# Retention and a gelu MLP on one core: the first w_in part triggered earlier, M1 of the first chunk begun on two batches, two loads put ahead of the last w_out part

## Chip, cores and metric

The kernel runs on one NeuronCore of one Trainium2 chip. The metric is the device time of one execution in microseconds (us). Times inside the kernel are us from the start of the profiled span.

## What is computed

For 4 batches (`B`), 8 heads (`H`), 768 steps (`S`) and a head width of 64 (`D`), a retention recurrence with one decay per head, and then a two-layer MLP with a tanh gelu on the 3072 rows of width 512 that it gives:

```python
for t in range(S):
    state = gamma[None, :, None, None] * state + np.einsum('bhd,bhe->bhde', k[:, :, t], v[:, :, t])
    y[:, :, t] = scale * np.einsum('bhd,bhde->bhe', q[:, :, t], state)
x = np.ascontiguousarray(attn_out.transpose(0, 2, 1, 3)).reshape(B * S, H * D)
h = x @ w_in                                          # 512 x 2048
g = 0.5 * h * (1.0 + np.tanh(c * (h + 0.044715 * h * h * h)))
out = (g @ w_out).astype(np.float32)                  # 2048 x 512
```

All inputs and outputs are float32; the kernel works in float16 on the matmul side.

## The kernel before

**Chunks.** The 768 steps are cut into six chunks of 128. For each chunk and batch the recurrence becomes matmuls. `prep1` (L146) scales or casts a loaded 128x512 tile of q, k or v to float16, on the engine that is named in its first argument (VE = VectorE, AC = ScalarE, PO = GpSimd). `mm_T` (L183) transposes q and k of one batch on TensorE and `ev_T` (L192) copies the result out of PSUM. `mm_A` (L202) forms the scores and `ev_A` (L216) masks them, always on VectorE. `mm_yc`, `mm_yi` (L223, L238) form the outputs, `ev_Y` (L251) writes them as columns of the MLP's input x. `mm_s`, `ev_S` (L260, L274) carry the state to the next chunk. I call these steps T, A, Y and S. A chunk's x has 512 columns, 128 per batch.

**M1 and M2.** M1 is x times w_in and the gelu. It has 16 blocks of 128 features. `moe1` (L366) does one block on all 512 columns with four matmuls. `moe1_two` (L371) does a pair of blocks, `fp`, on a range of columns, so that it can start while later batches are not there yet: `t01` is batches 0 and 1, `t2` batch 2, `t3` batch 3. Each leaves its sum in a PSUM bank of the tag "h", of which there are two, and ScalarE takes it out with the gelu (L363). M2 is g times w_out, done with seven products of half size instead of eight, on sums of g and of w_out that VectorE or GpSimd form beforehand (`g_sums` L396, `w_sums` L389). For chunk 0 the products are cut into the pieces of `units_0` (L515), so that parts of w_out can be used as they arrive; a table (L734) says what work of chunk 1 is put after which piece.

**Weights.** w_in and w_out are each loaded in four parts. Each part is read as 1 MB of float32 and lands as 512 KB of float16. The loads are issued from GpSimd[...] (`load_w_in` L328, `load_w_out` L336). Part i of w_in holds blocks 4i to 4i+3; part i of w_out holds the same blocks of the second layer.

**Order.** There is no scheduler: each engine runs its instructions in the order in which the code records them (`manual_schedule`), and waits by semaphores. A DMA is issued by a queue's engine in that same order: `load1(AC, ...)` on ScalarE's, the loads of `nc.sync` on SyncE's, `load1(PO, ...)` and the weights on GpSimd's. Twelve loads of 256 KB bring q, k, v of the four batches of chunk 0; they are issued from SyncE and ScalarE in the first 10 us. `spin(n)` (L114) puts n matmuls on zeros into TensorE's queue, where it would otherwise have nothing to do.

**The opening.** After the twelve loads, GpSimd prepares k of batches 0 and 1, issues w_in part 0, prepares k of batch 2, issues w_in parts 1 to 3, prepares k and q of batch 3, issues the four parts of w_out and then loads of chunk 1 (`loads`, L604). TensorE does T, A, Y of batches 0 and 1, T and A of batch 2, T of batch 3, and then begins M1 with pair 0 on batches 0 and 1 (L672), with A, Y and S of the late batches between its pieces. From block 6 on, M1 goes by full blocks (L696).

Of the kernel before, what the change touches and what calls it, by code (L numbers as in the profile page):

```python
# [16 lines left out]
def kernel(  # L17
# [16 lines left out]
    NF = d_ff // 128  # L34
# [44 lines left out]
    def ld_tile(nm, c, b):  # L79
        if (nm, c, b) not in raw:  # L80
            raw[nm, c, b] = ld.tile([128, H, Dh], F32, tag=f"{nm}32", bufs=6 if nm == "v" else 8, name=f"{nm}32")
        return raw[nm, c, b]
# [31 lines left out]
    def spin(n):  # L114
        ps = bank("h", shape=(128, 512), name="spin_ps")
        for _ in range(n):
            nc.tensor.matmul(
                out=ps, lhsT=zero[:, 0:128], rhs=zero, start=True, stop=True
            )
# [20 lines left out]
    def copy_on(eng, out, in_):  # L140
        if eng is nc.scalar:
            eng.copy(out=out, in_=in_)  # L142
        else:
            eng.tensor_copy(out=out, in_=in_)

    def prep1(eng, nm, c, b):  # L146
        if nm == "v":
            t = pre.tile([128, H, Dh], F16, tag="v16", bufs=2 * B, name="v16")
        else:
            if (c, b) not in qk16:  # L150
                qk16[c, b] = pre.tile([128, 2, H, Dh], F16, tag="qk16", bufs=2 * B, name="qk16")
            t = qk16[c, b][:, "qk".index(nm)]
        src = ld_tile(nm, c, b)
        if (nm == "v") == (c < 1):
            copy_on(eng, t, src)
        else:
            col = OQ if nm == "q" else OK
            eng.tensor_tensor(  # L158
                out=t,
                in0=src,  # L160
                in1=cst[:, col:col + H].unsqueeze(2).broadcast_to([128, H, Dh]),
                op=ALU.mult,
            )
        h16[nm, c, b] = t

    def pair(t, hp):
        return t[:, 2 * hp:2 * hp + 2]
# [8 lines left out]
    def bank(tag, dt=F32, shape=(128, NHP, 128), name="ps"):  # L176
        return psum.tile(list(shape), dt, tag=tag, bufs=BANKS[tag], name=name)

    def qkT_tile(c, b):
        qkT[c, b] = att.tile([128, 2, NHP, 128], F16, tag="qkT", bufs=2 * B, name="qkT")  # L180
        return qkT[c, b]

    def mm_T(c, b):  # L183
        ps = bank("att", F16, (128, 2, NHP, 128), "qkT_ps")
        for i, nm in enumerate("qk"):
            for hp in range(NHP):
                nc.tensor.transpose(  # L187
                    out=ps[:, i, hp], in_=pair(h16[nm, c, b], hp), identity=iden
                )
        pss["T", c, b] = ps  # L190

    def ev_T(c, b, eng=nc.vector):  # L192
        copy_on(eng, qkT_tile(c, b), pss.pop(("T", c, b)))
# [8 lines left out]
    def mm_A(c, b):  # L202
        t = qkT[c, b]
        ps = [bank("att", name=f"a_ps{j}") for j in range(2)]
        for hp in range(NHP):
            for j in range(2):
                nc.tensor.matmul(  # L207
                    out=ps[j][:, hp],
                    lhsT=t[j * 64:(j + 1) * 64, 1, hp],
                    rhs=t[j * 64:(j + 1) * 64, 0, hp],  # L210
                    start=True,
                    stop=True,
                )
        pss["A", c, b] = ps

    def ev_A(c, b):  # L216
        ps = pss.pop(("A", c, b))
        for j in range(2):
            s = att.tile([128, NHP, 128], F16, tag=f"a{j}", name=f"a_sb{j}")
            nc.vector.tensor_tensor(out=s, in0=ps[j], in1=mask[:, j], op=ALU.mult)  # L220
            a_sb[c, b, j] = s

    def mm_yc(c, b, tag):  # L223
        y_ps = pss["Y", c, b] = bank(tag, name="y_ps")
        if c == 0:
            return

        for hp in range(NHP):
            nc.tensor.matmul(  # L229
                out=y_ps[:, hp],  # L230
                lhsT=st[:, b, hp].rearrange("p j d -> p (j d)"),
                rhs=qkT[c, b][:, 0, hp],
                start=(hp == 0),
                stop=False,
                skip_group_check=True,
            )
# [88 lines left out]
    NO = 4  # L325
    w_out_sb = [const.tile([128, NF // NO, d_model], F16, name=f"w_out{i}") for i in range(NO)]

    def load_w_in(i):  # L328
        nc.gpsimd.dma_start(
            out=w_in_sb[i],  # L330
            in_=moe_w_in.rearrange("(kc p) n -> p kc n", p=128)[
                :, :, w_in_at[i] * 128:(w_in_at[i] + w_in_n[i]) * 128
            ],
        )

    def load_w_out(i):  # L336
        n = NF // NO
        nc.gpsimd.dma_start(
            out=w_out_sb[i],
            in_=moe_w_out.rearrange("(fc p) n -> p fc n", p=128)[:, i * n:(i + 1) * n],  # L340
        )
# [3 lines left out]
    def moe1_mm(c, fc, out, t0, t1):  # L345
        wi, wr = w_in_of[fc]
        for kc in range(NHP):
            nc.tensor.matmul(  # L348
                out=out,
                lhsT=w_in_sb[wi][:, kc, wr * 128:(wr + 1) * 128],  # L350
                rhs=xT[c][:, kc, t0:t1],
                start=(kc == 0),
                stop=(kc == NHP - 1),
                skip_group_check=True,
            )

    def g_tile(c, fc):
        if (c, fc // 8) not in g_sb:
            g_sb[c, fc // 8] = gp.tile([128, 8, B * C], F16, tag=f"g{fc // 8}", name="g")
        r = fc % 8 // 2 * 2  # L360
        return g_sb[c, fc // 8][:, r:r + 2]

    def gelu(out, in_):  # L363
        nc.scalar.activation(out=out, in_=in_, func=AF.Gelu_apprx_tanh, scale=1.0)  # L364
# [6 lines left out]
    def moe1_two(c, fp, t0, t1):  # L371

        h_ps = bank("h", shape=(128, 2, B * C // 2), name="h_ps")
        for r in range(2):
            moe1_mm(c, 2 * fp + r, h_ps[:, r, 0:t1 - t0], t0, t1)
        gelu(g_tile(c, 2 * fp)[:, :, t0:t1], h_ps[:, :, 0:t1 - t0])
# [12 lines left out]
    def w_sums(i):  # L389
        t = {j: t_w[j][:, 2 * i:2 * i + 2] for j in t_w}  # L390
        tt(nc.vector, t[1], w_q(i, 0, 1), w_q(i, 0, 0), ALU.subtract)
        tt(nc.vector, t[3], w_q(i, 1, 1), w_q(i, 0, 1), ALU.subtract)
        tt(nc.vector, t[2], w_q(i, 1, 1), t[1], ALU.subtract)
        tt(nc.vector, t[4], w_q(i, 1, 0), t[2], ALU.subtract)

    def g_sums(eng, c, f0, f1, p0=0, p1=2):  # L396
        g = g_sb[c, f0 // 4].rearrange("p (f r) (a b t) -> p r b f a t", r=2, a=2, b=2)
        i = f0 % 4
        q = {
            (r, b): g[:, r, b][:, i:i + f1 - f0, p0:p1] for r in range(2) for b in range(2)  # L400
        }
        t = {j: s_g[j][:, f0:f1, p0:p1] for j in s_g}
        tt(eng, t[1], q[0, 1], q[1, 1], ALU.add)
        tt(eng, t[2], t[1], q[0, 0], ALU.subtract)
        tt(eng, t[3], q[0, 0], q[0, 1], ALU.subtract)
        tt(eng, t[4], q[1, 0], t[2], ALU.subtract)
# [197 lines left out]
    def loads(eng, c, *what):  # L604
        for nm, b in what:
            load1(eng, nm, c, int(b))
# [7 lines left out]
    VE, AC, PO, SY = nc.vector, nc.scalar, nc.gpsimd, nc.sync  # L614
    half = 2 * C
# [5 lines left out]
    prep1(VE, "q", 0, 0)  # L621
    prep1(PO, "k", 0, 0)
    prep1(AC, "v", 0, 0)
    mm_T(0, 0)
    ev_T(0, 0, AC)
    load1(AC, "k", 0, 3)
# [11 lines left out]
    ev_Y(0, 0, AC)  # L638
    prep1(VE, "q", 0, 2)

    load_w_in(0)
    prep1(PO, "k", 0, 2)
    for i in range(1, 4):
        load_w_in(i)
    prep1(PO, "k", 0, 3)
    prep1(PO, "q", 0, 3)
    for i in range(NO):
        load_w_out(i)
    loads(PO, 1, "q0", "k0", "q1", "k1", "v0", "v1", "q2", "k2")
    mm_A(0, 1)  # L650
    ev_A(0, 1)
    spin(2)
# [10 lines left out]
    mm_A(0, 2)  # L663
    ev_A(0, 2)
    prep1(AC, "v", 0, 3)
    spin(4)
    mm_T(0, 3)
    ev_T(0, 3)


    t01, t2, t3 = (0, half), (half, half + C), (half + C, 2 * half)
    moe1_two(0, 0, *t01)  # L672
    mm_A(0, 3)
    ev_A(0, 3)
    mm_yc(0, 2, "o")
    mm_yi(0, 2)
    ev_Y(0, 2, AC)
    moe1_two(0, 1, *t01)
    moe1_two(0, 0, *t2)
    moe1_two(0, 1, *t2)  # L680
    mm_yc(0, 3, "o")
    mm_yi(0, 3)
    mm_s(0, (2, 3))
    ev_Y(0, 3)
    ev_S(0, (2, 3))
    moe1_two(0, 2, *t01)
    for fp in range(2):
        moe1_two(0, fp, *t3)
    moe1_two(0, 2, half, 2 * half)

    nc.gpsimd.tensor_copy(out=dec[0:1, 0, 0:1], in_=w_out_sb[3][0:1, 0, 0:1])
    nc.sync.dma_start(out=dec.rearrange("p h t -> p (h t)"), in_=dec_h.ap())
    loads(PO, 1, "q3", "k3", "v2", "v3")
    loads(SY, 2, *[x + str(b) for nm in ("qk", "v") for b in range(B) for x in nm])

    for fc in range(6, NF):  # L696
        moe1(0, fc)
        if fc == 7:
            g_sums(VE, 0, 0, 2)
            w_sums(0)  # L700
        if fc == 8:
            g_sums(VE, 0, 2, 4)
        if fc == 11:
            w_sums(1)
            g_sums(VE, 0, 4, 6)
# [23 lines left out]
    def mm_Y(b, tag):  # L729
# [4 lines left out]
        units_0(),  # L734
        {
            0: [(w_sums, 2), (g_sums, VE, 0, 6, 8)],
            1: [(w_sums, 3)],
            3: [(preps, 1, 0)],
            5: [(att_T, 0)],
            6: [(preps, 1, 1)],  # L740
            7: [(att_1A, 0)],
            8: [(att_T, 1), (preps, 1, 2)],
# [96 lines left out]
```

## Time and profile before

The time before is 206.78 us, the median of 3 runs (206.63 to 207.46). The profiled span is 204.9 us.

| stretch (us) | TensorE busy | DMA moved (GB/s) | what TensorE does |
|---|---|---|---|
| 0 to 4 | 2.74 of 4 | 130 | spin |
| 4 to 8 | 1.86 of 4 | 288 | T of batch 0, spin |
| 8 to 12 | 3.75 of 4 | 288 | A, T, Y of batches 0, 1, spin |
| 12 to 16 | 3.77 of 4 | 239 | T and A of batch 2, Y and S of batches 0, 1, spin |
| 16 to 20 | 3.77 of 4 | 208 | T of batch 3, M1 begins at 16.73 |
| 20 to 24 | 3.65 of 4 | 206 | M1 in pieces, Y and S of batch 3 |
| 24 to 30 | 6.00 of 6 | 207 | M1 in full blocks |
| 34 to 40 | 5.76 of 6 | 342 | M2 of chunk 0 |

A page lists the busy time of each engine (PE is TensorE, DVE VectorE, ACT ScalarE, POOL GpSimd, SP SyncE), the DMA queues (q0 is GpSimd's, q1 SyncE's, q10 ScalarE's), the chain of work that ended last, and the costliest groups of instructions. A busy TensorE in the first 16 us is partly spin, which computes nothing. Further views used here are the timeline of an engine (start, length, what, and in brackets the idle time before it with what ended it) and the DMA view of a short stretch, which gives the issues in it and the time from issue to landing.

### The profile page before, as it was taken

Reading aid. Unit: us, or ns where it says so; the run is one execution under the profiler, and the core shown is the slowest. Engines: PE = TensorE matmul, PEld = TensorE weight load, DVE = VectorE, ACT = ScalarE, POOL = GpSimd, SP = SyncE. Lnnn points to the kernel's source line nnn. Section 1 sums busy time; section 2 is a strip of 40 time slices with the busy share of each in tenths; the row PEclk is TensorE's granted clock in tenths of the full one; section 3 lists DMA queues with packets and bytes.
Section 4 is the critical chain, followed back from the end, with each engine's and each line's share of the span. In section 5 each row is a group of like instructions: output and inputs, shape, how many; then the busy total and the mean of one; then the engine's idle time right before and its main releaser. Section 6 shows DMA issues by size and latency. Waiting matters only on the chain.

```text
span 204.9 us, 4576 instructions
## 1 busy us (share of the span) xinstructions
PE 196.4 (96%) x1868; PEld 136.2 (66%) x1868; DVE 103.1 (50%) x239; ACT 102.2 (50%) x180; POOL 121.9 (60%) x124
## 2 busy tenths in 40 slices
PE   5798999999999999999999999999999999999993
PEld 1456747888687888644788644778644788544882
DVE  5346669679970459601379502289402284053420
ACT  2375464563479418466635365635366411566321
POOL 0599323944099999569997269996279980200000
PEclk9999999999999999999999999999999999999999
DMA  7999999999986899999982999442420000400004
GB/s 164 288 260 207 206 207 267 348 318 218 333 187 87 190 239 248 176 278 272 251 170 55 162 350 253 109 102 57 142 110 3 2 3 0 205 0 3 0 21 184
DMA packets 87092, 34.21 MB, mean 167 GB/s; under 512 B 80032, under 2 KB 84512, under 8 KB 87072
## 3 DMA queue, kind: packets, MB, share of 16 engines
q1 hardware_dynamic: 73920, 19.25, 44.0%
q0 software_dynamic: 6624, 12.58, 23.8%
q10 hardware_dynamic: 6528, 2.10, 4.1%
q8 instruction: 14, 0.23, 0.5%
q14 instruction: 6, 0.05, 0.1%
HBM read 27.63 MB, written 6.29 MB: 166 GB/s over the span
## 4 chain that ended last, share of the span: by engine, by line
PE 87%; DMA 7%; DVE 3%; ACT 1%; ACTq 1%; POOL 1%; issue 0%
PE h_ps L348 40%; PE o_ps L456 31%; DMA w_in<-in_moe_w_in_dram 4%; PE o_ps L525 3%; PE y_ps L242 3%; PE a_ps L207 3%; DMA k<-in_k_dram 3%; PE o_ps L558 2%; PE y_ps L229 2%; DVE st L285 2%; PE s_ps L266 1%; PE qkT_ps L187 1%; DVE a_sb L220 1%; ACT g L364 1%; ACTq L85 1%; POOL qk L158 1%
## 5 line engine op out<-in xcount | busy, mean ns | idle before, releaser
L348 PE MATMUL h_ps<-xT,w_in 128*128 128x512 f16 (+2 forms) x488 | 87.7, 334 | 0.5 <-ACT g L364 0.5
L364 ACT ACTIVATE g<-h_ps 128x512 f16<-128x512 f32 (+1 forms) x98 | 57.5, 589 | 33.1 <-PE h_ps L348 32.9
L348 PEld LDWEIGHTS <-w_in 128*128 128x128 f16 x488 | 45.4, 98 | 37.8 <-issue 2.2
L220 DVE TENSOR_TENSOR a_sb<-a_ps,mask 128x512 f16<-128x512 f32 x48 | 30.1, 683 | 43.7 <-PE a_ps L207 43.7
L387 POOL TENSOR_TENSOR s_g<-g 128x512 f16<-128x512 f16 x32 | 36.8, 1152 | 11.6 <-ACT g L364 11.6
L456 PEld LDWEIGHTS <-s_g 128*128 128x128 f16 x320 | 30.2, 98 | 4.7 <-POOL s_g L387 0.7
L456 PE MATMUL o_ps<-t_w,s_g 128*128 128x256 f16 x240 | 28.1, 273 | 0.0
L456 PEld LDWEIGHTS <-g 128*128 128x128 f16 x240 | 23.5, 98 | 3.6
L158 POOL TENSOR_TENSOR v<-v,cst 128x512 f16<-128x512 f32 x20 | 20.4, 1044 | 4.6 <-DMA v<-in_v_dram 3.7
L285 DVE SCALAR_TENSOR_TENSOR st<-st,cst,s_ps 64x128 f16<-64x128 f16 (+1 forms) x80 | 20.6, 318 | 0.7 <-PE s_ps L266 0.5
L387 POOL TENSOR_TENSOR s_g<-s_g,g 128x512 f16<-128x512 f16 x16 | 18.4, 1152 | 1.3
L387 POOL TENSOR_TENSOR s_g<-g,s_g 128x512 f16<-128x512 f16 x16 | 18.4, 1153 | 0.0
L456 PE MATMUL o_ps<-w_out,g 128*128 128x256 f16 x160 | 18.3, 273 | 0.0
L489 POOL DMA_DIRECT2D out_dram<-o_sb x8 | 5.9, 737 | 17.9 <-DVE o_sb L387 17.0
L258 DVE TENSOR_TENSOR xT<-y_ps,dec 128x512 f16<-128x512 f32 x20 | 13.0, 685 | 4.0 <-PE y_ps L242 3.8
L142 ACT CAST qk<-q 128x512 f16<-128x512 f32 x20 | 12.4, 620 | 2.9 <-DMA q<-in_q_dram 2.9
L387 DVE TENSOR_TENSOR s_g<-g 128x512 f16<-128x512 f16 x16 | 6.7, 421 | 11.8 <-ACT g L364 11.8
L485 ACT COPY o_sb<-o_ps 128x512 f32<-128x512 f32 (+1 forms) x5 | 2.7, 543 | 19.9 <-PE o_ps L456 17.6
L142 ACT CAST qk<-k 128x512 f16<-128x512 f32 x20 | 12.4, 620 | 0.4 <-DMA k<-in_k_dram 0.3
L387 DVE TENSOR_TENSOR o_sb<-o_ps,s_p 128x512 f32<-128x512 f32 (+1 forms) x7 | 4.3, 616 | 15.4 <-ACT qk L142 8.0
L479 ACT COPY s_u<-o_ps 128x512 f32<-128x512 f32 (+1 forms) x6 | 3.1, 514 | 17.2 <-PE o_ps L456 12.0
L456 PE MATMUL o_ps<-w_out,s_g 128*128 128x256 f16 x80 | 9.6, 273 | 0.0
(62 smaller groups left out, 179.9 us busy)
## 6 DMA issues: line engine op xcount, KB each, us to landing
out_dram<-o_sb POOLq DMA_DIRECT2D x10, 512.0 KB, 5.1
k<-in_k_dram SPq DMA_DIRECT2D x18, 256.0 KB, 4.2
q<-in_q_dram SPq DMA_DIRECT2D x18, 256.0 KB, 4.6
v<-in_v_dram SPq DMA_DIRECT2D x18, 256.0 KB, 4.5
w_in<-in_moe_w_in_dram POOLq DMA_DIRECT2D x4, 512.0 KB, 9.1
w_out<-in_moe_w_out_dram POOLq DMA_DIRECT2D x4, 512.0 KB, 14.4
q<-in_q_dram POOLq DMA_DIRECT2D x4, 256.0 KB, 11.3
k<-in_k_dram POOLq DMA_DIRECT2D x4, 256.0 KB, 9.6
```

The costliest lines, as they stand in the source:

```text
L142: eng.copy(out=out, in_=in_)
L158: eng.tensor_tensor(out=t, in0=src, in1=cst[:, col:col + H].unsqueeze(2).broadcast_to([128, H, Dh]), op=ALU.mult,)
L207: nc.tensor.matmul(out=ps[j][:, hp], lhsT=t[j * 64:(j + 1) * 64, 1, hp], rhs=t[j * 64:(j + 1) * 64, 0, hp], start=True, stop=True,)
L220: nc.vector.tensor_tensor(out=s, in0=ps[j], in1=mask[:, j], op=ALU.mult)
L242: nc.tensor.matmul(out=y_ps[j * 64:(j + 1) * 64, hp], lhsT=h16["v", c, b][:, 2 * hp + j], rhs=a_sb[c, b, j][:, hp], start=(c == 0), stop=True,
L258: nc.vector.tensor_tensor(out=x, in0=ps, in1=dec, op=ALU.mult)
L285: nc.vector.scalar_tensor_tensor(out=t[:, :, hp], in0=t[:, :, hp], scalar=cst[sl, OG + hp:OG + hp + 1], in1=s_ps[sl, :, hp], op0=ALU.mult, ...
L348: nc.tensor.matmul(out=out, lhsT=w_in_sb[wi][:, kc, wr * 128:(wr + 1) * 128], rhs=xT[c][:, kc, t0:t1], start=(kc == 0), stop=(kc == NHP - ...
L364: nc.scalar.activation(out=out, in_=in_, func=AF.Gelu_apprx_tanh, scale=1.0)
L387: eng.tensor_tensor(out=out, in0=in0, in1=in1, op=op)
L456: nc.tensor.matmul(out=po, lhsT=lhs(c, lk, fp, a), rhs=rhs(rk, fp), start=(new and fp == 0 and (last or a == 0)), stop=(stop and fp == NP ...
L525: nc.tensor.matmul(out=ps[k][:, a], lhsT=lhs(0, lk, fp, a), rhs=rhs(rk, fp), start=(first and fp == 0 and a == 0), stop=(stop and fp == NP ...
```

## The change

It regroups the opening, in three pieces.

- **w_in part 0** is issued from GpSimd right behind the preparation of k of batch 0, and M1 begins with pairs 0 and 1 (the blocks of part 0) on batches 0 and 1, ahead of T of batch 3. `spin(4)` before T of batch 3 goes. The rest of M1's split pairs is put in a new order: pairs 0 to 3 are now done in pieces, and full blocks begin at block 8 (before: 6). It is meant to have matmuls for TensorE as soon as the first weights and two batches are there.
- **q of batch 3** is prepared on GpSimd before w_in parts 1 to 3 are issued; k of batch 3 stays behind them.
- **q and k of batch 0 of chunk 1** are loaded ahead of the last part of w_out. In the table of the second stage their preparation and T come one piece earlier, and the sums on w_out part 3 come later, behind T. Two g sums stand together at block 8.

```diff
     prep1(VE, "q", 0, 0)
     prep1(PO, "k", 0, 0)
     prep1(AC, "v", 0, 0)
+    load_w_in(0)
     mm_T(0, 0)
...
-    load_w_in(0)
     prep1(PO, "k", 0, 2)
+    prep1(PO, "q", 0, 3)
     for i in range(1, 4):
         load_w_in(i)
     prep1(PO, "k", 0, 3)
-    prep1(PO, "q", 0, 3)
-    for i in range(NO):
+    for i in range(3):
         load_w_out(i)
-    loads(PO, 1, "q0", "k0", "q1", "k1", "v0", "v1", "q2", "k2")
+    loads(PO, 1, "q0", "k0")
+    load_w_out(3)
+    loads(PO, 1, "q1", "k1", "v0", "v1", "q2", "k2")
...
     prep1(AC, "v", 0, 3)
-    spin(4)
-    mm_T(0, 3)
-    ev_T(0, 3)
...
     moe1_two(0, 0, *t01)
-    mm_A(0, 3)
-    ev_A(0, 3)
+    moe1_two(0, 1, *t01)
     mm_yc(0, 2, "o")
     mm_yi(0, 2)
     ev_Y(0, 2, AC)
-    moe1_two(0, 1, *t01)
+    mm_T(0, 3)
+    ev_T(0, 3)
     moe1_two(0, 0, *t2)
     moe1_two(0, 1, *t2)
+    mm_A(0, 3)
+    ev_A(0, 3)
+    moe1_two(0, 2, *t01)
+    moe1_two(0, 3, *t01)
     mm_yc(0, 3, "o")
     mm_yi(0, 3)
     mm_s(0, (2, 3))
     ev_Y(0, 3)
     ev_S(0, (2, 3))
-    moe1_two(0, 2, *t01)
-    for fp in range(2):
+    for fp in (2, 3):
+        moe1_two(0, fp, half, 2 * half)
+    for fp in (0, 1):
         moe1_two(0, fp, *t3)
-    moe1_two(0, 2, half, 2 * half)
...
-    for fc in range(6, NF):
+    for fc in range(8, NF):
         moe1(0, fc)
-        if fc == 7:
+        if fc == 8:
             g_sums(VE, 0, 0, 2)
+            g_sums(VE, 0, 2, 4)
             w_sums(0)
-        if fc == 8:
-            g_sums(VE, 0, 2, 4)
...
             0: [(w_sums, 2), (g_sums, VE, 0, 6, 8)],
-            1: [(w_sums, 3)],
-            3: [(preps, 1, 0)],
-            5: [(att_T, 0)],
+            2: [(preps, 1, 0)],
+            4: [(att_T, 0)],
+            5: [(w_sums, 3)],
             6: [(preps, 1, 1)],
```

## The prediction

> **What bounds the kernel now.** I read the busy shares first, then the chain of waits, then the timelines of the queues and the DMA view over short stretches. The page's parts 1 and 4:
>
> ```profile
> PE 196.4 (96%) x1868; PEld 136.2 (66%) x1868; DVE 103.1 (50%) x239; ACT 102.2 (50%) x180; POOL 121.9 (60%) x124
> PE 87%; DMA 7%; DVE 3%; ACT 1%; ACTq 1%; POOL 1%; issue 0%
> ```
>
> TensorE is the bound nearly everywhere, and the 7% of DMA lies at the start. So the change can only move the moment at which M1 of chunk 0 ends (33.10 us); what follows is a TensorE chain that shifts with it. The chain of waits, columns start, length, what:
>
> ```profile
> 7.87 1.05 POOL qk L158
> 8.92 7.76 DMA w_in<-in_moe_w_in_dram
> 16.73 1.05 PE h_ps L348 x8
> ...
> 22.98 10.11 PE h_ps L348 x56
> 33.10 5.24 PE o_ps L525 x48
> ```
>
> M1 cannot start before w_in part 0 lands (16.68). From there to 33.10 are 16.4 us, of which the 16 column blocks of M1 take 13.84 (0.865 each), A, Y and S of the late batches 1.4, and waits for gelu the rest. The timeline, rows of the issuing queues and GpSimd (start, length, what; in brackets the idle time before and what ended it):
>
> ```profile
> 5.34 1.04 POOL L158 TENSOR_TENSOR qk<-k,cst 128x512 f16<-128x512 f32 x1 [4.90 <-DMA k<-in_k_dram]
> ...
> 5.97 1.76 SPq L85 DMA_DIRECT2D q<-in_q_dram  x1
> ...
> 7.38 1.28 ACTq L85 DMA_DIRECT2D k<-in_k_dram  x1
> ...
> 7.77 1.76 SPq L85 DMA_DIRECT2D v<-in_v_dram  x1
> ...
> 8.92 0.93 POOL L329 DMA_DIRECT2D w_in<-in_moe_w_in_dram  x1
> ...
> 10.62 1.05 POOL L158 TENSOR_TENSOR qk<-k,cst 128x512 f16<-128x512 f32 x1 [0.78 <-DMA k<-in_k_dram]
> ...
> 11.63 2.30 POOL L329 DMA_DIRECT2D w_in<-in_moe_w_in_dram  x3
> ```
>
> The three rows of SPq and ACTq are q, k and v of batch 3. Their times to landing, in the DMA view of a stretch that holds one issue each, and below them part 0:
>
> ```profile
> q<-in_q_dram SPq DMA_DIRECT2D x1, 256.0 KB, 6.4
> k<-in_k_dram ACTq DMA_DIRECT2D x1, 256.0 KB, 5.9
> v<-in_v_dram SPq DMA_DIRECT2D x1, 256.0 KB, 6.4
> w_in<-in_moe_w_in_dram POOLq DMA_DIRECT2D x1, 512.0 KB, 7.8
> ```
>
> Issue plus this: q3 lands at 12.4, k3 13.3, v3 14.2, part 0 at 16.7: 0.9 us for a load of 256 KB, 2.5 for a part of w_in. In the stretch 9 to 12 us part 0 is issued, yet all packets are those of the two hardware queues: it waits for what was issued before it.
>
> **What the skill says.** "DMA: Bandwidth & Descriptors", Issuing engines are not separate DMA queues: all queues run on the same 16 engines. The trace agrees: early part 0 is paid for by what is queued behind it. The same page, Queues, rings and completion order, has each engine taking turns between queues packet by packet; this trace looks more like order of arrival (the stretch 9 to 12, above), and I go by the trace. "PSUM — Partial Sum Buffer", Engine vs sequencer instructions, says that ScalarE's, VectorE's and GpSimd's queues are strict FIFO: here an ACT cast or a POOL preparation that waits for a load holds all behind it. "TensorE: Matmul & The Clock Gate", Part 1, has the array's clock at half after an idle window of about 3.4 us; the trace shows it slow at the start (spin matmuls 0.46 us each, later 0.26) and has no such gap after.
>
> **The change, part by part.**
> *Part 0 triggered earlier.* It is issued after k of batch 0: at 5.34+1.04 = 6.38 and not 8.92. It then stands before k3 (7.38) and v3 (7.77), and behind q2, k2, v2. q3 (issued 5.97, but its issue lasts until 7.73[...]) is the open point. Near-ties elsewhere: on SP, k at 47.26 lands 3.9 later (51.2) and q at 48.11 lands 5.4 later (53.5), 2.3 apart where loads in a row are 0.9 apart; between came the 512 KB store that GpSimd issued at 48.40. So a load whose issue is still going (48.11 to 48.95) lets a GpSimd transfer issued 0.29 us after its start in before its last piece. q3's issue goes on 1.35 us past 6.38. I take it that the tail of q3 falls behind part 0: part 0 lands at 16.7 - 2x0.9 - a piece of 0.9, about 14.6; q3 at 12.4+2.5 = 14.9, k3 at 15.8, v3 at 16.7.
>
> *POOL's order.* It is now k0, part 0, k1, k2, q3, parts 1 to 3, k3. q3's preparation moves before parts 1 to 3, and it now waits for a load that lands at 14.9 and not 12.4. It runs 14.95 to 16.0; parts 1 to 3 are issued at 16.0 to 18.3 (2.30 from the row), not 11.63 to 13.9; k3's preparation comes last, 18.3 to 19.35. Queued behind this wait is all of w_in and w_out. The DMA engines have work up to v3's last packet, 16.3. A GpSimd transfer on idle engines shows its first packets 1.25 us after its issue (stores at 146.12 and 174.67), so part 1 starts at 17.25, about 1 us of DMA time is lost, and it lands near 20.5 (it was 19.8: 11.63+8.2). What follows it comes 0.7 later.
>
> *TensorE's order.* A of batch 2 ends at 14.74 as before. Then:
> - Pairs 0, 1 on batches 0, 1, twice 0.87: 14.75 to 16.5. spin(4) is gone; it filled time in which nothing was ready, so that is worth nothing by itself.
> - ACT casts v3 ahead of the first gelu and now waits for it: 16.75 to 17.35, two gelus to 18.2, Y of batch 2 evacuated at 18.7. TensorE did Y of batch 2 at 17.0 to 17.35 (its masked scores are ready at 16.97, as before).
> - T of batch 3 waits for k3's preparation: 19.35 to 19.8. Here TensorE stands 2.0 us.
> - Pairs 0, 1 on batch 2: 0.9, to 20.7. A of batch 3: 0.33, to 21.05.
> - Pairs 2, 3 on batches 0, 1 (part 1 there since 20.5): to 22.8. Y and S of batch 3: 0.7, to 23.45. Its x comes from DVE at 23.85, so 0.4 of waiting.
> - Pairs 2, 3 on batches 2, 3: to 25.6. Pairs 0, 1 on batch 3: 0.9 and some 0.2 for a PSUM bank of "h": 26.7.
> - Eight full columns at 0.865: 33.6.
> Before, the same point was 33.10: +0.5 us. The start won 2.0, the stand for k3 gave it back, and T of batch 3 (0.45) and the longer ACT queue ate the rest.
>
> *q0, k0 of chunk 1 before the last w_out part; DVE sums and preparations moved in the opening of M2.* Same bytes, so w_out part 3 lands two loads of 0.77 later than at 35.3, and with the 0.7 above at 37.6. Its first reader, the rest of the first product, stood at 38.62 and will at 39.1: hidden by TensorE. The sums on that part follow T of batch 0 on DVE: 39.0 to 40.5, read at about 41.0; hidden, but close. q0 and k0 come 1.5 us earlier than they would have (36.1 and 36.9), where T at 38.17 did not wait; nothing gained. The two g sums drawn together at block 8 lie on DVE, which then waits for w_out anyway (1.9 us). All nought.
>
> Sum: 206.78 + 0.5 = 207.3 us.
>
> **Rivals.**
> *q3 wholly ahead of part 0.* It lands at 12.4; its preparation ends 13.5, parts 1 to 3 are issued to 15.8 while the DMA engines are busy, k3 is prepared at 16.9. T of batch 3 stands at 17.35 without waiting, x of batch 2 comes at 18.7, and the same list ends at 32.6: -0.5, so 206.3. For it: q3 starts its issue 0.4 us before part 0; against it: the store at 48.40.
> *The stand costs more.* Part 0 gets in even before k2 or v2, which then delays A of batch 2 itself by up to 2.5 us, or the stand of 2.0 us slows the clock of the array for the next stretch. The opening's half-speed stretch cost about 0.2 us for each 512-wide matmul; a few microseconds of it are worth 1 us. 208.3. Against it: k2 and v2 were issued at 4.17 and 6.11, and the gap is short of the stated window.
> *The early start carries.* If v3 and k3 are not held back by the whole 2.5 us, ACT is free at 15.4, pairs follow each other, and M1 ends near 31.8, held only by part 1 at 19.8 plus 12.0 of work behind it: -1.3, so 205.5. Against it: the bytes have to go somewhere.
>
> **How the numbers follow.** Chances: forecast 0.58, q3 ahead 0.18, stand costs more 0.15, early start carries 0.09. 0.5% is 1.03 us, so the bounds are 205.75 and 207.81. Slower: 0.15 and a fifth of the forecast, whose terms (part 1 between 19.9 and 21.2) spread by 0.6: 0.26. Faster: 0.09 and a little of the q3 case: 0.11. Same: 0.63. The range runs from the q3 case and a bit below it, 206.0, to the costly stand, 208.3.
>
> **What would show it.** In the changed profile: part 0 issued at 6.4 and landing at 14 to 15; q3's preparation on GpSimd waiting to about 14.9; parts 1 to 3 issued from 16.0; a dip of DMA near 16.5; TensorE idle about 2 us before T of batch 3, ended by GpSimd; M1's last column ending near 33.6. If q3 is prepared at 12.4, the q3 case holds. I am wrong altogether if something after 34 us differs, such as a wait for w_out part 3.

## The result, and the profile after

The changed kernel takes 209.93 us (median of 6 runs, 209.07 to 211.24), the kernel before 206.78 us (6 runs, 206.63 to 207.86): ratio 1.014, 95% interval 1.0098 to 1.0182 (the ratios here are estimates of their own with an interval, not quotients of the medians). So it is slower, and by more than the forecast of 207.3; it lies outside the range of 206.0 to 208.3. In the profiled executions the span goes from 204.9 to 207.5 us, 2.6 more. The medians differ by 3.15, and what follows explains the 2.6 alone: the three longest executions of the changed kernel (spans of 208.5, 208.5 and 209.5) have no trace.

In the three runs with part 0 early and q3 prepared behind parts 1 to 3 (e1, f1, g1 below) the times fall into two groups, 6 to 8 us apart (f1: 12 of 20 executions from 207.00 to 209.44, the other 8 from 211.47 to 215.59), and their ratios are those of the lower group.

The page's parts 1 and 4, as shown for before:

```profile
PE 195.9 (94%) x1872; PEld 136.5 (66%) x1872; DVE 103.1 (50%) x239; ACT 102.3 (49%) x180; POOL 122.1 (59%) x124
PE 84%; DMA 7%; DVE 3%; SPq 2%; ACT 1%; POOL 0%; issue 0%
```

TensorE's busy time is what it was (195.9, before 196.4), its share of the chain fell from 87% to 84%. The work is the same; TensorE stands (is idle and waits) longer. The chain of waits (start, length, what) says for what:

```profile
5.91 10.00 DMA q<-in_q_dram
15.98 0.99 POOL qk L158
16.96 5.42 DMA w_in<-in_moe_w_in_dram
22.43 1.92 PE h_ps L348 x16
...
28.09 7.51 PE h_ps L348 x40
35.60 4.37 PE o_ps L525 x40
```

Before, the chain went through part 0 of w_in (issued 8.92, 7.76 long) into M1 at 16.73. Now it goes through the load of q3, ten microseconds long, GpSimd's preparation of it, and then part 1 of w_in. M1 ends at 35.60, before at 33.10: +2.50. From there to the end are 171.9 us (207.5 less 35.6), before 171.8 (204.9 less 33.1). So the whole loss of the profiled execution is in the end of M1.

GpSimd's timeline (start, length, what; in brackets the idle time before and what ended it):

```profile
6.50 0.93 POOL L329 DMA_DIRECT2D w_in<-in_moe_w_in_dram  x1
...
15.98 1.04 POOL L158 TENSOR_TENSOR qk<-q,cst 128x512 f16<-128x512 f32 x1 [4.22 <-DMA q<-in_q_dram]
16.96 2.30 POOL L329 DMA_DIRECT2D w_in<-in_moe_w_in_dram  x3
19.26 1.07 POOL L158 TENSOR_TENSOR qk<-k,cst 128x512 f16<-128x512 f32 x1
```

GpSimd waits 4.22 us for q3, with parts 1 to 3 of w_in queued behind that wait: they go out at 16.96, before at 11.63. The DMA view of three stretches that hold the issues of part 0, q3 and part 1 gives the times to landing, in the last column:

```profile
w_in<-in_moe_w_in_dram POOLq DMA_DIRECT2D x1, 512.0 KB, 8.2
q<-in_q_dram SPq DMA_DIRECT2D x1, 256.0 KB, 10.0
w_in<-in_moe_w_in_dram POOLq DMA_DIRECT2D x1, 512.0 KB, 5.4
```

Part 0 lands at 14.72 (before 16.68), q3 at 15.91 (12.4), part 1 at 16.96 + 5.42 = 22.4 (19.84). Part 1 is issued on DMA engines that are running dry, and still takes 5.4 us. The view by windows shows it; columns are the window and its length, busy us of each engine with the count of instructions, TensorE's clock, the DMA share and GB/s. Of before:

```profile
15.00:18.00 3.00, 2.67 (x28) 1.54 (x26) 2.53 (x4) 1.14 (x3) 3.00 (x4) 1.00 1.25 209
18.00:22.00 4.00, 3.76 (x67) 3.21 (x64) 2.18 (x4) 2.25 (x5) 2.75 (x4) 1.00 1.24 204
```

and of after:

```profile
15.00:18.00 3.00, 2.70 (x28) 1.92 (x27) 1.98 (x3) 1.67 (x5) 2.02 (x3) 1.00 0.56 126
18.00:22.00 4.00, 1.61 (x28) 1.34 (x28) 0.69 (x1) 1.66 (x5) 4.00 (x6) 1.00 0.89 144
```

The DMA share, which reads about 1.25 here when the engines are all fed, falls to 0.56 between 15 and 18 us, and TensorE is busy 1.61 of the 4 us from 18 to 22, before 3.76. TensorE's timeline there:

```profile
17.49 0.40 PE L187 MATMUL qkT_ps<-iden,qk 128*128 128x128 f16 x4
20.39 0.40 PE L187 MATMUL qkT_ps<-iden,qk 128*128 128x128 f16 x4 [2.50 <-POOL qk L158]
...
22.43 1.92 PE L348 MATMUL h_ps<-xT,w_in 128*128 128x256 f16 x16 [0.42 <-DMA w_in<-in_moe_w_in_dram]
...
35.44 1.91 PE L525 MATMUL o_ps<-w_out,g 128*128 128x256 f16 x16
```

T of batch 3 stands 2.50 us for k3 in the middle, and pairs 2, 3 then wait 0.42 more for part 1. The last line is the first matmul of M2. Which of the two waits sets the end can't be read from this alone: the first is longer, but it may be time that would be spent waiting for part 1 anyway.

### The profile page after: what moved, and what is told of

The parts are those of the page before. It is cut to its first block, busy times and chain, and to the rows that moved or that the text cites. A ratio compares the mean times of both kernels' runs of the same rounds, so it can differ in the third digit from the quotient of the medians.

```text
span 207.5 us, 4583 instructions
## 1 busy us (share of the span) xinstructions
PE 195.9 (94%) x1872; PEld 136.5 (66%) x1872; DVE 103.1 (50%) x239; ACT 102.3 (49%) x180; POOL 122.1 (59%) x124
## 4 chain that ended last, share of the span: by engine, by line
PE 84%; DMA 7%; DVE 3%; SPq 2%; ACT 1%; POOL 0%; issue 0%
PE h_ps L348 39%; PE o_ps L456 30%; DMA q<-in_q_dram 5%; PE o_ps L525 3%; PE y_ps L242 3%; PE a_ps L207 3%; DMA w_in<-in_moe_w_in_dram 3%; PE o_ps L558 2%; PE y_ps L229 2%; SPq L85 2%; DVE st L285 2%; PE s_ps L266 1%; PE qkT_ps L187 1%; DVE a_sb L220 1%; POOL qk L158 0%
## 5 line engine op out<-in xcount | busy, mean ns | idle before, releaser
L348 PEld LDWEIGHTS <-w_in 128*128 128x128 f16 x496 | 46.0, 98 | 37.7 <-issue 1.8
L387 POOL TENSOR_TENSOR s_g<-g 128x512 f16<-128x512 f16 x32 | 36.9, 1153 | 11.5 <-ACT g L364 11.5
L489 POOL DMA_DIRECT2D out_dram<-o_sb x8 | 5.9, 739 | 17.4 <-DVE o_sb L387 16.5
L142 ACT CAST qk<-q 128x512 f16<-128x512 f32 x20 | 12.4, 620 | 1.7 <-DMA q<-in_q_dram 1.7
L142 ACT CAST qk<-k 128x512 f16<-128x512 f32 x20 | 12.4, 619 | 1.1 <-DMA k<-in_k_dram 0.9
L187 PE MATMUL qkT_ps<-iden,qk 128*128 128x128 f16 x64 | 6.1, 242 | 4.6 <-POOL qk L158 2.5
```

The lines of the kernel that those rows point to most:

```text
L187: nc.tensor.transpose(out=ps[:, i, hp], in_=pair(h16[nm, c, b], hp), identity=iden)
L348: nc.tensor.matmul(out=out, lhsT=w_in_sb[wi][:, kc, wr * 128:(wr + 1) * 128], rhs=xT[c][:, kc, t0:t1], start=(kc == 0), stop=(kc == NHP - ...
L387: eng.tensor_tensor(out=out, in0=in0, in1=in1, op=op)
```

## The experiments

The theory after this reading: what costs the time is the place of q3's preparation in GpSimd's queue, since it holds back part 1. Rivals: the long stand for k3 costs it; the early part 0 costs it by itself; the new order of TensorE costs even with early loads.

**Is it the stand for k3, or part 1?** In e8_k3_between, k3 is prepared right behind the issue of part 1, ahead of parts 2 and 3.

```diff
-    for i in range(1, 4):
-        load_w_in(i)
+    load_w_in(1)
     prep1(PO, "k", 0, 3)
+    for i in range(2, 4):
+        load_w_in(i)
```

> The changed kernel with one edit: k of batch 3 is prepared between w_in part 1 and parts 2, 3. In the changed kernel part 1 landed 5.4 us after its issue although the DMA engines were empty, with few packets until GpSimd had issued all three parts. Theory A (issuing the next parts at once slows the delivery of part 1): with 1.1 us of other work behind it, part 1 lands 3.7 to 4.2 after its issue, at about 20.8, T of batch 3 at 18.9, M1 ends near 33.7, time 207.3. Theory B (a GpSimd transfer of this form on empty engines is slow to start, whatever follows): part 1 lands 5 us or more after its issue, near 22.2, M1 ends at 35 or later, time 208.7 to 209.5.

Measured: 211.0 us (209.28 to 211.04, 4 runs), ratio 1.0177 (1.0129 to 1.0224). TensorE's timeline of this run:

```profile
18.57 0.88 PE L187 MATMUL qkT_ps<-iden,qk 128*128 128x128 f16 x8
...
22.56 1.92 PE L348 MATMUL h_ps<-xT,w_in 128*128 128x256 f16 x16 [1.87 <-DMA w_in<-in_moe_w_in_dram]
```

T of batch 3 comes 1.8 us earlier and waits for nothing, and pair 2 begins at 22.56 instead of 22.43. The stand only moved: 1.87 us for part 1 in place of 2.50 for k3 and 0.42 for part 1. So the stand for k3 costs nothing by itself; part 1 is the bound. Part 1 was issued alone at 17.11 and landed at 22.52, 5.4 us again, so the issue of the next parts right behind it is not what makes it slow. What remains common to both runs is a start on engines that have run dry; that this is the reason is not shown, for in both GpSimd is also at work right behind the issue (here with the preparation of k3, from 17.94 to 18.99).

**Is it the place of q3's preparation?** Both e1_q3_behind_parts and f1_q3_behind_parts put it back behind parts 1 to 3, with everything else as in the changed kernel.

```diff
     prep1(PO, "k", 0, 2)
-    prep1(PO, "q", 0, 3)
     for i in range(1, 4):
         load_w_in(i)
     prep1(PO, "k", 0, 3)
+    prep1(PO, "q", 0, 3)
```

> The changed kernel with one edit: q of batch 3 is prepared on GpSimd behind w_in parts 1 to 3 and k of batch 3, as before. Theory (GpSimd's wait for q3 at 11.8 to 16.0 us holds parts 1 to 3): parts 1 to 3 are issued from 11.8, part 1 lands at 19.5 to 20 instead of 22.4, T of batch 3 runs at about 18.2 to 18.7, M1 of chunk 0 ends at 32.9 to 33.3, and the time is 206.3 to 207.0. Rival (the early part 0 itself costs, because it pushes q3, k3, v3 back): part 1 may come earlier, but the time stays at 208.5 or more.

> The edit of e1_q3_behind_parts again (q of batch 3 prepared behind w_in parts 1 to 3 and k of batch 3), for a trace with TensorE at its usual speed. Theory: parts 1 to 3 are issued at about 11.5 and the DMA engines have no gap, so part 1 lands at 19.5 to 20.4 instead of 22.4, T of batch 3 runs at about 18.5. If v of batch 3 lands by 17.5, ScalarE's first gelu is done at 18.1, M1 ends near 33 and the time is 206.5 to 207.5. If the tail of v is split behind part 1, as in e2_part0_alone (last piece at 20.1), ScalarE's cast of v holds the gelus, M1 ends at 35 to 36 and the time is 209 to 210. The rival (the early part 0 costs by itself, wherever q3 stands) expects 209 or more even with v3 on time.

Measured: e1 ratio 1.0057 (1.0031 to 1.0082, from 9 of 20 executions, 207.06 to 209.42); its profiled execution took 1103.59 us, and its trace is not used. f1, the same kernel again: 207.99 us in the lower group (12 of 20 executions; the median of all 20 is 208.53), ratio 1.0045 (1.0025 to 1.0065), profiled span 205.7. TensorE's timeline of f1:

```profile
18.23 0.62 PE L187 MATMUL qkT_ps<-iden,qk 128*128 128x128 f16 x8 [1.21 <-POOL qk L158]
...
20.32 1.92 PE L348 MATMUL h_ps<-xT,w_in 128*128 128x256 f16 x16
...
33.33 1.91 PE L525 MATMUL o_ps<-w_out,g 128*128 128x256 f16 x16
```

With parts 1 to 3 issued from 11.55, part 1 lands at 20.25, pair 2 begins at 20.32, and the first M2 matmul stands at 33.33; in the changed kernel that one stands at 35.44, before at 32.93. One moved line takes back 2.11 of 2.51 us in the traced executions, and the ratio falls from 1.014 to 1.0045. That is the main cause, shown. It is no gain over all executions: the mean of f1's 20 is 210.59 us, that of the changed kernel's six 209.94. And in the trace 0.4 us of the loss remains although part 0 is early.

**Why does an early part 0 gain nothing even then?** From the start of pair 2 on batches 0, 1 to the first M2 matmul the new order takes 13.01 us in the changed kernel (22.43 to 35.44), 13.02 in e8 (22.56 to 35.58), 13.01 in f1 (20.32 to 33.33): a constant. In the kernel before it is 11.68 (21.25 to 32.93), by its TensorE timeline:

```profile
21.25 1.49 PE L348 MATMUL h_ps<-xT,w_in 128*128 128x256 f16 x16
...
32.93 1.91 PE L525 MATMUL o_ps<-w_out,g 128*128 128x256 f16 x16
```

The new order has 1.33 us more of work and waits behind part 1. Both orders have the same thirteen blocks of M1 behind this point, pairs 0, 1 on batch 3 among them; what the new one has besides is Y and S of batch 3 (0.7 us), which in before came ahead of pair 2, and a wait of 0.54 for the x of batch 3. To be even with before, pair 2 must begin at 32.93 - 13.01 = 19.92; part 1 landed at 19.84 in before, and nowhere before 19.75 in any run here. Early bytes for part 0 don't make part 1 earlier, as it has the same loads ahead of it; by this reckoning the best to be had is about even. Three runs ask about this. In f3_part0_late (and e3_part0_late, the same edit) part 0 is back at its old place, and TensorE's new order and the third piece stay.

```diff
     prep1(AC, "v", 0, 0)
-    load_w_in(0)
     mm_T(0, 0)
...
     prep1(VE, "q", 0, 2)
 
+    load_w_in(0)
     prep1(PO, "k", 0, 2)
```

> The changed kernel with one edit: w_in part 0 is issued where it was before, behind the second k. Theory: q3 lands at 12.4 again, its preparation ends at 13.5, parts 1 to 3 are issued at 13.5 to 15.8 while the DMA engines are still busy, part 1 lands at 19.8, T of batch 3 doesn't wait for GpSimd, M1 starts at 16.7 and ends at about 33.3 to 33.6; time 206.9 to 207.3. Rival (the new order of M1's pieces or the chunk 1 loads cost by themselves): 208.5 or more.

> The edit of e3_part0_late again (w_in part 0 at its old place, all else as in the changed kernel), for a trace with TensorE at its usual speed. Theory (the displaced loads and the late parts are the whole loss): q3 lands at 12.4, parts 1 to 3 are issued from 13.5, part 1 lands at 19.8 to 20.5, M1 starts at 16.7 and ends at 33.3 to 33.7; 207.0 to 207.5. Rival (the new order of M1 costs too): M1 ends at 34.5 or later with part 1 landed by 20.5, time 208.3 or more.

Measured: e3 207.9, 209.47 and 210.6 us, ratio 1.0116 (1.0049 to 1.0183); its profiled execution took 502.26 us, and its trace is not used. f3: 209.29 us (8 runs), ratio 1.0083 (1.0046 to 1.0119), profiled span 207.9. q3 lands at 12.48 again and part 1 at 20.47, M1 starts at 16.92, pair 2 at 21.32, and the first M2 matmul stands at 34.33: 13.01 behind pair 2 once more, 1.40 later than before. The new order costs that by itself when part 0 is not early, as the rival had it. The rest of this run's loss lies elsewhere, and is taken up below.

In e2_part0_alone the opposite: the kernel before, with only the trigger of part 0 moved.

```diff
     prep1(AC, "v", 0, 0)
+    load_w_in(0)
     mm_T(0, 0)
...
     prep1(VE, "q", 0, 2)
 
-    load_w_in(0)
     prep1(PO, "k", 0, 2)
```

> The kernel before with one edit: w_in part 0 is issued behind the first k; order of M1 and of GpSimd's other work as before. Theory: part 0 lands at 14.7 but q3 and k3 at about 16; in this order T of batch 3, with k3 and q3 prepared at 16.1 to 18.2, stands ahead of M1, so M1 starts at about 18.7 instead of 16.7 and the time is 208.5 to 209. Part 1 lands at 19.5 to 20. Rival (an earlier part 0 pays by itself): M1 starts at 15 to 16 and the time is 205 to 206.5.

Measured: 210.14 us (208.9 to 211.09, 4 runs), ratio 1.017 (1.013 to 1.0211), profiled span 207.1: the first M2 matmul at 35.13, 2.2 later than before. TensorE's timeline:

```profile
18.48 0.62 PE L187 MATMUL qkT_ps<-iden,qk 128*128 128x128 f16 x8 [2.98 <-POOL qk L158]
18.94 1.04 PE L348 MATMUL h_ps<-xT,w_in 128*128 128x256 f16 x8
```

Part 0 lands at 14.81, and nobody uses it: T of batch 3 stands ahead of M1 and waits 2.98 us for k3 and q3, which moved back to make room. M1 starts at 18.94, before at 16.73. Neither the early part nor the order is of use alone, and together they come near to even only if part 1 is issued in time (f1).

The last of the three, f6_mended, gives the idea its best case: parts 1 to 3 issued right behind k2, q3 behind them on GpSimd, k3 on VectorE, and the cast of v3 behind the gelu of pair 2, so that no preparation holds a load or another.

```diff
     prep1(PO, "k", 0, 2)
-    prep1(PO, "q", 0, 3)
     for i in range(1, 4):
         load_w_in(i)
-    prep1(PO, "k", 0, 3)
+    prep1(PO, "q", 0, 3)
...
-    prep1(AC, "v", 0, 3)
+    prep1(VE, "k", 0, 3)
...
     moe1_two(0, 2, *t01)
+    prep1(AC, "v", 0, 3)
     moe1_two(0, 3, *t01)
```

> The changed kernel with GpSimd's and ScalarE's waits on batch 3 taken out of the way: w_in parts 1 to 3 issued behind k of batch 2, q of batch 3 prepared on GpSimd behind them, k of batch 3 on VectorE behind the scores of batch 2, the cast of v of batch 3 behind the gelu of pair 2. Theory: part 0 lands at 14.8, part 1 at 19.8 to 20.4, T of batch 3 runs at about 17.9, TensorE waits once for part 1, M1 ends at 31.9 to 32.6 instead of 33.1, time 205.5 to 206.3. Rival (an early part 0 can't pay, since the same bytes are ahead of part 1 and the stragglers of the split loads are waited for): M1 ends at 33 or later, 206.7 or more.

Measured: 208.73 us (208.71 to 209.27, 4 runs), ratio 1.0067 (1.0041 to 1.0093). Part 1 lands at 20.36, pair 2 begins at 20.40, the first M2 matmul stands at 33.79 (13.39 later, with a wait of 0.32 for v3's cast in it), 0.86 later than before. So the rival of the expectation holds: even so the early part 0 did not pay in this order. (The other half of this run's loss, a wait of 0.88 us in M2, is that of the next part.)

**The third piece.** f4_chunk1_alone is the kernel before with only q0, k0 of chunk 1 ahead of w_out part 3, and the sums on that part (w_sums(3)) behind T.

```diff
-    for i in range(NO):
+    for i in range(3):
         load_w_out(i)
-    loads(PO, 1, "q0", "k0", "q1", "k1", "v0", "v1", "q2", "k2")
+    loads(PO, 1, "q0", "k0")
+    load_w_out(3)
+    loads(PO, 1, "q1", "k1", "v0", "v1", "q2", "k2")
...
-            1: [(w_sums, 3)],
-            3: [(preps, 1, 0)],
-            5: [(att_T, 0)],
+            2: [(preps, 1, 0)],
+            4: [(att_T, 0)],
+            5: [(w_sums, 3)],
```

> The kernel before with the third piece alone: q0 and k0 of chunk 1 loaded ahead of the last w_out part, preparation and T one piece earlier, the sums on w_out part 3 behind T. Theory: hidden by TensorE, M1 unchanged; w_out part 3 lands at 36.9, q0 at 33.6; time within 0.3 of before. Rival (the later part 3 is waited for in M2): TensorE idle near 38 to 40 and 0.5 to 1.5 us more.

Measured: 207.79 us (206.44 to 211.06, 20 runs; before 207.09), ratio 1.0029 (1.0004 to 1.0054). Hardly more than nought, and the profiled execution was the longest of the twenty (211.06), with k3 landing at 16.92, so it says little on this piece: its first M2 matmul stands at 37.29, late before the piece begins. But f3 and f6 showed a wait that neither before nor after has. VectorE's timeline of f3:

```profile
39.95 2.31 DVE L387 TENSOR_TENSOR t_w<-w_out 128x512 f16<-128x512 f16 x2
42.18 1.72 DVE L387 TENSOR_TENSOR t_w<-w_out,t_w 128x512 f16<-128x512 f16 x2
```

and TensorE's of the same run:

```profile
43.49 0.38 PE L558 MATMUL o_ps<-t_w,s_g 128*128 128x256 f16 x2 [1.39 <-DVE t_w L387]
```

The sums on w_out part 3 took 2.31 and 1.72 us for the two pairs, and TensorE waited 1.39 us for them (0.88 in f6). In before the same pairs took 0.76 and 0.88, in the changed kernel 0.75 and 0.88. What differs is GpSimd beside them: in f3 it issues v loads until 40.9 and then prepares two v tiles, 40.91 to 43.15; in the changed kernel the sums run 41.06 to 42.5, before that preparation starts at 44.19. g3_part0_late_sums_early is f3 with the sums drawn earlier and nothing else.

```diff
             0: [(w_sums, 2), (g_sums, VE, 0, 6, 8)],
+            1: [(w_sums, 3)],
             2: [(preps, 1, 0)],
             4: [(att_T, 0)],
-            5: [(w_sums, 3)],
```

> f3_part0_late (the kernel after with w_in part 0 at its old place) with one edit: the VectorE sums on w_out part 3 are drawn ahead of T of batch 0 of chunk 1 (between the first and the third block), not behind it; loads as in f3. Theory: in f3 the two pairs of sums took 2.31 and 1.72 us because they ran from 39.95 to 43.9 beside GpSimd's v preparation and load issues (39.1 to 43.2); drawn near 37.2, ahead of that preparation, they take 0.75 and 0.88 again, the wait of 1.39 us of the second product goes, and the time falls by 1.4 from 209.3 to about 207.9. Rival: the sums are slow whatever they run beside (fresh data of w_out part 3), then they stay over 1.5 us a pair and push the preparation of chunk 1's q, k and T behind them: 209 or more.

Measured: 207.95 us (207.82 to 208.0, 6 runs), ratio 1.0049 (1.0033 to 1.0065; before 206.82), 1.34 less than f3 (1.07 when each is set against its own before, 207.09 and 206.82), profiled span 206.2. VectorE's timeline:

```profile
38.24 0.76 DVE L387 TENSOR_TENSOR t_w<-w_out 128x512 f16<-128x512 f16 x2
38.91 0.88 DVE L387 TENSOR_TENSOR t_w<-w_out,t_w 128x512 f16<-128x512 f16 x2
```

The sums are fast again and the wait in M2 is gone, though GpSimd issues loads beside them (37.98 to 41.5); its preparation of v starts at 41.51. The first M2 matmul stands at 34.26, as in f3. So the late sums cost 1.1 to 1.4 us where they fall beside that preparation, and nothing in the changed kernel itself, whose later M1 moved both apart.

g1_q3_behind_no_third undoes the third piece in f1.

```diff
-    for i in range(3):
+    for i in range(NO):
         load_w_out(i)
-    loads(PO, 1, "q0", "k0")
-    load_w_out(3)
-    loads(PO, 1, "q1", "k1", "v0", "v1", "q2", "k2")
+    loads(PO, 1, "q0", "k0", "q1", "k1", "v0", "v1", "q2", "k2")
...
-            2: [(preps, 1, 0)],
-            4: [(att_T, 0)],
-            5: [(w_sums, 3)],
+            1: [(w_sums, 3)],
+            3: [(preps, 1, 0)],
+            5: [(att_T, 0)],
```

> The kernel after, with q of batch 3 prepared behind the parts of w_in (as in f1_q3_behind_parts) and the third piece undone: w_out part 3 loaded ahead of q0, k0 of chunk 1, its sums early on VectorE. Theory: the third piece has no part in the end of M1, so the first M2 matmul is at 33.3 as in f1, and only the 0.33 us of waiting that f1 shows in M2 at 44.72 goes: about 208.2 (f1: 208.53, before: 207.1), sums on t_w 0.75 and 0.88. Rival: the third piece is worth nothing whichever way, so 208.5 and the same wait.

Measured: 207.28 us in the lower group (12 of 23 executions, 207.11 to 208.07; the other 11 from 213.75 to 219.69), ratio 1.0026 (1.0014 to 1.0038), f1 1.0045 (1.0025 to 1.0065): the intervals overlap, and whether the third piece costs f1 the 0.33 us that it waits in M2 at 44.72 stays open. The profiled execution took 215.4 us, so it can't answer for the first M2 matmul at 33.3; it shows one way in which such an execution gets long. ScalarE's timeline, and below it TensorE's:

```profile
19.83 0.62 ACT L142 CAST v<-v 128x512 f16<-128x512 f32 x1 [4.36 <-DMA v<-in_v_dram]
```

```profile
21.96 1.86 PE L348 MATMUL h_ps<-xT,w_in 128*128 128x128 f16 x16 [2.53 <-ACT xT L142]
...
24.30 3.50 PE L348 MATMUL h_ps<-xT,w_in 128*128 128x256 f16 x16
```

v3's first DMA engine is done at 16.39, its last at 19.81, just ahead of part 1 (20.55): its last pieces came in among the packets of part 1, which was issued later. ScalarE waits 4.36 us for it with the gelus and x of batch 2 queued behind, TensorE stands 2.53 us, and then runs slow: the 16 matmuls that take 1.92 us in f1 take 3.50, and the page's row of the granted clock has one slice of 5 tenths there. Pair 2 starts 4.0 later than in f1, the first M2 matmul 5.6 later (38.89). Whether the other long executions are of this kind is not shown: this is the only one with a trace. "TensorE: Matmul & The Clock Gate", Part 1, has the array at half clock after an idle window of about 3.4 us. Here two stands of 1.36 and 2.53 us lie within 4.5 us, neither as long as that, and the single stand of 2.50 in the changed kernel was followed by no such slice. Which rule holds was not tried.

**A version of its own.** The runs say that M1 can begin earlier only if a load moves back that is needed late, and that part 1 must not move. v3 is such a load. In g6_v3_behind_part0, the kernel before, only this load moves: from SP, ahead of part 0, to GpSimd, behind it. g5_v3_behind_pair0_first also lets the first pair of M1 run ahead of T of batch 3, and the second ahead of A of batch 3.

```diff
-    load1(nc.sync, "v", 0, 3)
...
     load_w_in(0)
+    load1(PO, "v", 0, 3)
     prep1(PO, "k", 0, 2)
```

and in g5 besides:

```diff
-    spin(4)
-    mm_T(0, 3)
-    ev_T(0, 3)
     moe1_two(0, 0, *t01)
-    mm_A(0, 3)
-    ev_A(0, 3)
+    mm_T(0, 3)
+    ev_T(0, 3)
     mm_yc(0, 2, "o")
     mm_yi(0, 2)
     ev_Y(0, 2, AC)
     moe1_two(0, 1, *t01)
+    mm_A(0, 3)
+    ev_A(0, 3)
```

> The kernel before with one load moved: v of batch 3 is issued on GpSimd behind w_in part 0, not on SP ahead of it; TensorE's order as before. It trades places only with a load that is needed late. Theory (order of arrival sets the landings): part 0 lands one load earlier, near 15.8 instead of 16.7, v3 near 16.7, q3 and k3 unchanged; T of batch 3 still waits for GpSimd's preparations to about 16.1 and stands ahead of M1, so M1 starts near 16.6 and little is gained: 206.7 (before 206.8 to 207.1). Rival: v3's cast on ScalarE, which stands ahead of the first gelu, now comes late and delays it: 207.3.

> The load as in g6_v3_behind_part0 and the first pair of M1 columns put ahead of T of batch 3, Y of batch 2 and the second pair between T and A of batch 3 (the idea of the changed kernel's second piece, with q3 and w_in part 1 left where they were before). Theory: M1 begins with part 0 near 15.9 instead of 16.73, part 1 at about 19.9 is not waited for (pair 2 near 20.6), and M1 ends 0.6 to 0.8 us earlier: about 206.2, ratio 0.997. Rival: v3's cast ahead of the first gelu or part 1 holds what was won: 206.8 to 207.3.

Measured against 206.95 of before (35 runs): g6 206.92 us (206.42 to 207.89, 14 runs), ratio 1.0002 (0.9983 to 1.0021); g5 206.47 us (206.18 to 207.48, 22 runs), ratio 0.9973 (0.9959 to 0.9987). TensorE's timeline of g5 (its line numbers are one less):

```profile
15.94 1.05 PE L347 MATMUL h_ps<-xT,w_in 128*128 128x256 f16 x8 [0.61 <-DMA w_in<-in_moe_w_in_dram]
16.82 0.61 PE L186 MATMUL qkT_ps<-iden,qk 128*128 128x128 f16 x8
...
20.48 0.38 PE L241 MATMUL y_ps<-a_sb,v 128*64 128x128 f16 x7 [0.20 <-DVE a_sb L219]
20.67 0.44 PE L265 MATMUL s_ps<-v,qk 128*64 128x64 f16 x16
21.04 1.49 PE L347 MATMUL h_ps<-xT,w_in 128*128 128x256 f16 x16
...
32.73 1.91 PE L524 MATMUL o_ps<-w_out,g 128*128 128x256 f16 x16
```

Part 0 lands at 15.89 and M1 begins at 15.94, 0.79 earlier than before. T of batch 3 then waits for nothing. But pair 2 begins at 21.04, only 0.21 earlier, since T of batch 3 (0.54) now stands behind the start of M1 and Y of batch 3 waits 0.20 for the masked scores; the first M2 matmul stands at 32.73, 0.20 earlier. The median gain is 0.48 us (0.3 to 0.85 by the interval). It beats both kernels, by a little. The traces don't tell why: in g6's profiled execution, with the load alone moved, that matmul stands at 32.67, and g6 gains nothing by its median.

## Why the prediction was wrong

The forecast's median was slightly slower, and that direction was right; but its likeliest outcome was the same time (0.63, against 0.26 for slower), and the size, +0.5, was far off: +2.5 at the end of M1. Two terms of the sum were mis-sized: the landing of q3, and with it the issue of part 1 (0.96 us late), and the time from this issue to the landing (0.92 us more). Point by point:

- *Part 0 issued at 6.38, in ahead of q3's tail, landing near 14.6*: right (6.50, 14.72). A of batch 2 wasn't held up (it starts at 14.57; before 14.41), which ends the part of the second rival that had part 0 ahead of k2 or v2. The first rival, q3 wholly ahead, is out: q3 landed at 15.91, not 12.4.
- *q3 at 14.9, k3 15.8, v3 16.7*: here a step failed. The last came right (16.90), and so did the bytes, but the tails of q3 and k3 came in together, at 15.91 and 16.13, and not one after the other. The sum let the loads land in the order of their arrival. The DMA view of the changed kernel from 14 to 15 us, with q3 on SyncE's queue (q1) and k3 on ScalarE's (q10), has both at the same rate:

```profile
q1 hardware_dynamic: 537, 0.14, 61.3%
q10 hardware_dynamic: 535, 0.14, 60.2%
```

  So the two queues took turns, which the prediction had named and set aside, and q3 finished together with k3, 1.0 later than reckoned. Nor was it only a tail that fell behind part 0: from 10.5 to 11.5 us the view counts 157 packets of part 0 and none of SyncE's queue, while in before q3 was under way by then (811 packets of that queue).
- *Parts 1 to 3 issued from 16.0, on engines that go idle about then*: they went out at 16.96, the same 1.0 later.
- *Part 1 on idle engines: first packets after 1.25 us, landing near 20.5*: this is the other step that failed. The start was sized from the stores, and 16.0 to 20.5 is 4.5 us; measured was 5.42 (5.4 in e8). The 20.5 doesn't follow from the terms beside it either: the 19.8 of before and about 1 us lost would have been 20.8. Between 16.5 and 18 us the DMA view counts 12 small packets, none of them GpSimd's, and in the next 1.5 us these, all of GpSimd's queue:

```profile
DMA packets 63, 0.06 MB, mean 43 GB/s; under 512 B 0, under 2 KB 63, under 8 KB 63
```

  Against 200 GB/s and more when the engines are fed ahead. The two terms, 0.96 and 0.92, make the 1.9 us by which part 1 missed 20.5.
- *TensorE stands 2.0 us for k3, and that stand is what gives the win back*: the stand was there, 2.50, but it was not the bound: e8 took it away and gained nothing. The sum had pair 2 start at 21.05, by TensorE's list, with part 1 in since 20.5. It started at 22.43, by part 1: 1.38 of the 2.00 us that the sum missed.
- *Pair 2 to the end of M1, 21.05 to 33.6*: 12.55 reckoned, 13.17 measured (22.43 to 35.60): the other 0.62, in small terms (the first pairs 0.10, the wait for x 0.14, what follows it 0.36). The sum did not set this stretch beside the same one of before, 11.85 (21.25 to 33.10). Side by side they show that whatever is won ahead of pair 2 must first pay for 0.7, by the measured value 1.3 us more behind it, and that part 1, which in before had 1.4 us of slack (19.84 against 21.25), is what the new order leans on.
- *The third piece at nought, hidden but close*: in the changed kernel right, the rest of the span being equal to 0.1 us. "Close" was right in the sense that f3, with M1 ending 1.1 us earlier, has a wait of 1.39 us from it, by a cause that the forecast did not have.
- *The stand slows the array's clock* (second rival): not in the profiled execution, whose clock stays at 1.00 from 18 to 22 us. The three longest executions of the changed kernel have a lower mean clock (0.975 to 0.984; the others 0.998 and 0.999), and none of them has a trace, so this stays open for them. It need not be the stand: in e8 and f3, traced at 0.984, the granted clock is 0.50 from 8 to 14 us and 1.00 from 16 us on, so what they lost lies ahead of any stand.
- *The early start carries* (third rival): out. It needed part 1 at 19.8 and 12.0 us of work behind it; in the changed kernel part 1 came at 22.4, and where it came at 20.25 (f1), 13.0 us stood behind it.

The mechanism that was forecast, a load pushed back by part 0 and a wait on GpSimd with w_in queued behind it, is what happened. Its price was set too low in one place, the landing of part 1, and there by two terms of a microsecond each. f1 shows the price of that wait as a whole: without it, 2.11 of the 2.51 us come back.

## What to carry to other kernels

A transfer that is triggered earlier takes its place from loads that are already under way, so ask who prepares those loads and what is queued behind that preparation; above all, look for a wait for a load that is queued ahead of the trigger of the next large transfer on the same engine: here it cost 2.1 us. When an order is changed, compare the stretch from the last input that can't come earlier to the end, in both orders: if it got longer, the new order can win only if that input comes earlier too. The gain that was to be had, 0.3%, took two steps together: the one load that is needed late moved back, and the first pair of M1 put ahead of T of batch 3. The load alone gave nothing (g6).

## What the runs showed of the hardware

- A part of w_in (512 KB, issued by GpSimd, packets of 1 KB) on engines that have run dry takes 5.4 us from issue to landing (after, e8). "DMA: Bandwidth & Descriptors", Anatomy of one DMA — SWDGE (gpsimd) path, gives a fit of 2.0 us plus bytes at 436 GB/s, an estimate of 3.2 us for the 512 KB that land and of 4.4 us for the 1 MB that is read; the measurement decides. Fed without a gap, such parts follow each other at 2.5 us (19.84 and 22.34 for parts 1 and 2 in before). In e8 no load was issued right behind it, so it is no effect of the next issue; what else makes it slow was not tried.
- VectorE's fp16 sums with both inputs in SBUF (0.42 us each alone) took 1.0 to 1.45 us each, six of the eight in f3 and f6, at or about GpSimd's preparation of v, and that preparation took 2.24 us for two in place of 2.05. "SBUF — State Buffer", Who interferes with whom, says that a VectorE instruction with two SBUF inputs and a GpSimd instruction that reads SBUF contend for one shared pair of ports, which is an exclusive lock, and infers that GpSimd's work to issue a load does not contend with such sums. g3 agrees: moved out of the preparation's way, beside load issues only, the sums took 0.42 each. That it is this lock is the page's explanation; the runs show only that moving them apart ends it. By the trace, a first sum was already slow in the last microsecond of the load issues ahead of the preparation (f1: 39.6 to 40.9); GpSimd's starts are rough, and this stays open.
- The last pieces of a load can come in long after the first, among the packets of a large transfer that was issued later: v3 in e2 was in on its first engine at 16.36, on its last at 20.06, in g1 at 16.39 and 19.81; k3 in f4, where part 0 is not early, at 14.38 and 16.92. In f1 v3 was in at 16.23 and 16.85. The price depends on who waits: in g1 ScalarE stood 4.36 us, in e2 M1 took no longer for it (18.94 to 35.13, 16.19 us; before 16.20). An order with tight landings is judged by its spread too.
- For a microsecond of the changed kernel (14 to 15) two queues shared the DMA engines evenly: 537 packets of SyncE's, 535 of ScalarE's; in the same microsecond of e2 514 and 514, of f1 549 and 549. Yet part 0 in before, issued at 8.92, moved no packet from 9 to 12 us while those two queues moved 3431. When queues share and when one waits for the others was not tried.
